# Sliding-window attention with an expert layer on one core: batch 0's q and k turned 128 rows at a time into two banks by position

## The chip, the cores and the metric

The kernel runs on one core of one Trainium2 chip. The metric is the device time in microseconds of one execution. Lower is better.

## The reference

Two computations follow each other. The first is causal attention in a sliding window of 64 positions, over 8 batches, 8 heads, 576 positions and a head width of 64. The second is a two-layer feed-forward block with SiLU over all 8 x 576 = 4608 rows.

```python
scores = scale * np.matmul(q, k.transpose(0, 1, 3, 2))
mask = (rel >= 0) & (rel < window)          # rel = row - column, window = 64
attn = softmax(np.where(mask, scores, -1e9))
x = (attn @ v).transpose(0, 2, 1, 3).reshape(4608, 512)
h = x @ w_in                                # 512 x 2048
out = (h * sigmoid(h)) @ w_out              # 2048 x 512
```

Inputs and output are fp32 in DRAM. The kernel computes in bf16 with fp32 accumulation.

## The kernel before, in words

**Order of work.** The program is unrolled. A planner (class `Plan`) holds a queue of operations for each class of work, each operation with an assumed duration on the engines that may run it, and plays the queues against each other. What it yields is a fixed order of instructions for every engine and the choice of engine and PSUM bank for each operation. On the chip each engine runs its list in that order and waits for semaphores.

**Names.** The four classes of work that matter here are loads (`dma`, `early`, `ld0`), `turn` and `lift` for batch 0, scores, exponent and values (`s`, `exp`, `pv`), and the feed-forward block (`moe`). PSUM has eight banks: `at0` to `at3` and `mp0` to `mp3`. Batch 0 may use all; later the scores use `at` and the feed-forward block `mp`.

**Batch 0's q and k.** Two heads have 1152 rows of 64. They are loaded so that each of the 128 partitions holds nine consecutive rows: `natb[p, 64*m + d]` is row 9p+m. Partitions 0 to 63 hold the first head, 64 to 127 the second. The first q and k come as fp32 by SyncE's queue and are cast by ScalarE (L236); the other six come by GpSimd's queue with a cast in flight (L230). Scores need the head width on the partitions, so TensorE turns these tiles against the identity (`turn_first`, L282), and a `lift` (L292) copies a bank into `qt` or `kt`. A turn handles four heads (two tiles `ws[0]`, `ws[1]`) of q or k; there are four turns and two lifts for each. In the bank the columns stand by m and then p; a lift puts them back in row order 9p+m, so it reads with a stride and writes in a row. Before the change, a bank held a pair of heads (one from each tile), and a lift filled one stretch of 576 columns of `qt` or `kt`.

**Batch 0's scores and values.** For each half `a` (four heads) and each group `g` of three blocks of 64 positions, `scores_first` adds a bias by two matmuls (L314) and makes twelve small matmuls (L322); the exponents run on ScalarE (L340); `values` makes 24 small matmuls (L352); VectorE inverts the sums, scales and transposes into `bridge` (L359, L362, L366). Filler matmuls (L586) stand where the planner expects TensorE to be idle before batch 0's exponents are done.

**The feed-forward block.** A tile is 512 rows. Its first layer (L372) multiplies w_in by `bridge`, SiLU runs on ScalarE (L378), and its second layer (L381) multiplies by w_out. For tile 0 the second layer goes through the 16 slices of w_out in order, four matmuls for each; w_out comes in eight loads of two slices (L267), issued by GpSimd between loads of batch 1 (L240, L255). Scores (L334) and values (L352) of batch 1 are placed between the second-layer matmuls of tile 0, and so on for the later batches.

Of the kernel before, what the change touches and what calls it, by code (L numbers as in the profile page):

```python
# [9 lines left out]
BF16 = mybir.dt.bfloat16  # L10
# [112 lines left out]
def kernel(ctx, tc, q, k, v, w_in, w_out, out):  # L123
    nc = tc.nc
    B, H, S, D = q.shape
# [11 lines left out]
    NK = 2  # L137
# [5 lines left out]
    NM0, MARGIN = 9, 1.3  # L143
# [8 lines left out]
    ident = keep.tile([128, 128], BF16, name="ident")  # L152
# [8 lines left out]
    natbs = [keep.tile([128, S], BF16, name=f"natb{i}") for i in range(NNB)]  # L161
    qt = [keep.tile([128, NP * S], BF16, name=f"qt{i}") for i in range(NK)]
    kt = [keep.tile([128, 64 + NP * S], BF16, name=f"kt{i}") for i in range(NK)]
# [9 lines left out]
    banks = [psum.tile([128, 512], FP32, name=f"at{i}") for i in range(4)]  # L173
    banks += [psum.tile([128, 512], FP32, name=f"mp{i}") for i in range(4)]

    p = Plan(
        {"at": range(4), "pv": range(4, 6), "mp": range(4, 8), "all": range(8)},
        rank=dict(prime=-8, early=-10, one=-9, first=-9, dma=-1, ld0=-1, st=-2, silu=-3, out=-2, pv=0, s=1, moe=99, warm=200, turn=2,
                  norm=0, inverse=0, bridge=0, exp=1, mask=1, lift=2, block=2, shift=2, cast=4, late=5, clear=9),
        rank0=dict(turn=-6, cast=-6, lift=-5, shift=-4.5, exp=-4, mask=-4, inverse=-3.5, norm=-3, bridge=-3.2),  # L180
        ahead=dict(s=-5.5, exp=-4.6, pv=-5.5, inverse=-4.3, norm=-4.2, bridge=-4.25),
    )
# [31 lines left out]
    def clear_k(i):  # L214
        nc.vector.memset(kt[i][:, 0:64].bitcast(FP32), 0.0)

    c_ident = p.add("one", {"POOL": 1.3}, const_ident)
    c_vv = [p.add("one", {"DVE": 0.25}, lambda _, i=i: clear_vv(i)) for i in range(NV)]
    c_k = [p.add("one", {"DVE": 0.15}, lambda _, i=i: clear_k(i)) for i in range(NK)]
# [9 lines left out]
    def load_first_cast(w, u, kk):  # L229
        nc.gpsimd.dma_start(out=natbs[w][:, 0:S], in_=two(u, kk))  # L230

    def load_first(i, kk):
        nc.sync.dma_start(out=nats[i][:, 0:2 * S].bitcast(FP32), in_=two(0, kk))

    def cast_first(e, i, w):
        copies[e](out=natbs[w][:, 0:S], in_=nats[i][:, 0:2 * S].bitcast(FP32))  # L236
# [33 lines left out]
        )  # L270


    def at_bf16(op, i=0):
        return banks[op["bank"][i]].bitcast(BF16)[:, 0:S]

    def turn_first(op, ws):

        for u in range(2):
            for m in range(NM0):
                for j in range(2):  # L280
                    r = slice(64 * j, 64 * j + 64)
                    nc.tensor.matmul(  # L282
                        banks[op["bank"][j]].bitcast(BF16)[64 * u:64 * u + 64, 64 * m:64 * m + 64],
                        lhsT=natbs[ws[u]][r, 64 * m:64 * m + 64], rhs=ident[r, r],
                        is_transpose=True, start=(m == 0), stop=(m == NM0 - 1),
                    )

    def place_one(b, pj, kk):
        return kt[b % NK][:, 64 + pj * S:64 + (pj + 1) * S] if kk else qt[b % NK][:, pj * S:(pj + 1) * S]

    def lift(e, op, pj, kk, i):
        copies[e](  # L292
            out=place_one(0, pj, kk).rearrange("x (p m) -> x p m", m=NM0),
            in_=at_bf16(op, i).rearrange("x (m p) -> x p m", m=NM0),
        )

    def shift_v(e, b, hf, a, z):
# [116 lines left out]
    def add_first_batch():  # L414
        got = {}
        for what, u in FIRST_LOADS:
            if what == "v":
                add_v_loads(0, [u], [c_vv[0]])
                continue
            kk = "qk".index(what)  # L420
            w = n_nat[1] % NNB
            n_nat[1] += 1
            if u == 0:
                i = n_nat[0] % NN
                n_nat[0] += 1
                ld = p.add("ld0", {"SP": 0.45}, lambda _, i=i, kk=kk: load_first(i, kk), dma=-0.15 if kk == 0 else 0.7)
                ca = p.add("cast", {"ACT": 0.7, "DVE": 0.56}, lambda e, i=i, w=w: cast_first(e, i, w), [ld])
                nat_free[i] = [ca]
            else:
                ca = p.add("early" if (what, u) in FIRST_LOADS[2:6] else "dma", {"POOL": 0.6}, lambda _, w=w, u=u, kk=kk: load_first_cast(w, u, kk), dma=0.8)  # L430
            got[what, u] = (w, ca)
            if (what, u ^ 1) not in got:
                continue
            a = u // 2
            ws, loaded = zip(*[got[what, 2 * a + i] for i in range(2)])
            tu = p.add("turn", {"PE": 0.7}, None, [*loaded, c_ident], lat=0.1, pool="all", nb=2)
            tu["fn"] = lambda _, tu=tu, ws=ws: turn_first(tu, ws)
            for i in range(2):
                x = 2 * a + i
                tu["untils"][i].append(p.add("lift", {"ACT": 0.64, "DVE": 0.75}, lambda e, tu=tu, x=x, kk=kk, i=i:  # L440
                                             lift(e, tu, x, kk, i), [tu, c_k[0]]))
                kq_done[(0, a)] = kq_done.get((0, a), []) + tu["untils"][i]

    def add_w_out(which):
# [23 lines left out]
    def add_v_loads(b, parts, busy):  # L468
        v_landed.setdefault(b, []).extend(
            p.add("dma", {"POOL": 1.0}, lambda e, part=part: load_v(e, b, part), busy, dma=1.1, lat=MARGIN * (b > 0)) for part in parts)  # L470
# [61 lines left out]
    def add_tile(j):  # L532
# [46 lines left out]
        free_gt.update(uses)  # L579

    add_first_batch()
    add_batch_v(0)


    def warm(op):
# [4 lines left out]
                 pool="all")  # L590
# [52 lines left out]
```

The softmax here doesn't subtract the row's maximum and nothing guards it: scores larger than these inputs give would overflow.

## Time and profile before

| what | value |
|---|---|
| median of 4 runs | 305.59 us (305.31 to 305.97) |
| the profiled execution | 305.62 us, of which the span is 303.8 us |
| TensorE matmuls, busy | 286.7 us (94% of the span) |
| VectorE, ScalarE, GpSimd, busy | 137.2, 172.2, 125.2 us |
| first-layer matmuls of tile 0 start | 20.70 us |
| second-layer matmuls of tile 0 start | 36.84 us |
| mean granted TensorE clock | 0.989 |

"Span" is the time from the first to the last instruction in the trace. PE is TensorE's matmuls, PEld its weight loads, DVE VectorE, ACT ScalarE, POOL GpSimd, SP SyncE. A row of a timeline begins with its start in us and the time it took; a number in square brackets is the idle time of the engine before it and what ended it. "issue" is idle time for which the profile shows no cause. TensorE works through its list in order, so a wait in one instruction holds up all behind it.

### The profile page before, as it was taken

The page shows a single profiled execution, that of the slowest core. Times are in us where ns is not written, and L with a number is a line of the kernel's source. Part 1 is how long each engine was busy: PE and PEld are TensorE (multiplying, and loading weights), DVE is VectorE, ACT ScalarE, POOL GpSimd, SP SyncE. Part 2 cuts the span into 40 slices and gives each one's busy share as a digit, 9 for nine tenths or more (in the row PEclk, how much of TensorE's full clock was granted, in tenths as well). Part 3 has the DMA queues.
Part 4 walks back from the last instruction along what each step waited for, and adds up shares of the span by engine and source line. Part 5 has one row for each costly group of instructions (what it writes and reads, how often), then busy time and mean ns, then how long its engine had stood idle before and what let it go on. Part 6 is the DMA issues. An engine that isn't in the chain of part 4 may idle for free.

```text
span 303.8 us, 8450 instructions
## 1 busy us (share of the span) xinstructions
PE 286.7 (94%) x3601; PEld 144.7 (48%) x3635; DVE 137.2 (45%) x329; ACT 172.2 (57%) x314; POOL 125.2 (41%) x177
## 2 busy tenths in 40 slices
PE   4969987999999999999999999999999999999996
PEld 2546444554544454445444454445445444444444
DVE  3474466752999098806970786055104520000000
ACT  4856662577357744775387628663667366226611
POOL 8967975969989898991320000000000000000000
PEclk9978999999999999999999999999999999999999
DMA  8999999999999999998290111002001110010012
GB/s 170 161 189 150 135 177 159 161 183 104 153 176 149 113 139 187 151 125 84 78 106 2 38 71 37 1 37 73 35 0 39 56 50 0 37 69 36 2 69 70
DMA packets 115238, 28.64 MB, mean 94 GB/s; under 512 B 104704, under 2 KB 110464, under 8 KB 115200
## 3 DMA queue, kind: packets, MB, share of 16 engines
q0 software_dynamic: 109440, 18.07, 78.9%
q1 hardware_dynamic: 5760, 10.03, 9.2%
q8 instruction: 28, 0.46, 0.6%
q14 instruction: 10, 0.08, 0.1%
HBM read 36.70 MB, written 9.44 MB: 152 GB/s over the span
## 4 chain that ended last, share of the span: by engine, by line
PE 82%; POOL 8%; DMA 5%; issue 3%; ACT 0%; POOLq 0%; ACTq 0%
PE mp L381 39%; PE mp L372 37%; DMA w_in_sb<-in_moe_w_in_dram 3%; PE at L334 3%; PE mp L352 3%; DMA w_out_sb<-in_moe_w_out_dram 2%; POOL vv L255 2%; POOL w_in_sb L261 2%; POOL nat L240 2%; POOL natb L230 1%; POOL w_out_sb L267 1%; PE at L352 1%; ACT g L378 0%; POOL ident L189 0%; ACT ot L387 0%
## 5 line engine op out<-in xcount | busy, mean ns | idle before, releaser
L372 PE MATMUL mp<-bridge,w_in_sb 128*128 128x512 bf16 (+3 forms) x624 | 130.0, 368 | 0.5 <-ACT g L378 0.4
L381 PE MATMUL mp<-w_out_sb,g 128*128 128x512 bf16 (+2 forms) x574 | 124.5, 367 | 5.3 <-issue 3.7
L378 ACT ACTIVATE g<-mp 128x512 bf16<-128x512 f32 (+3 forms) x156 | 86.3, 564 | 37.1 <-PE mp L372 36.1
L372 PEld LDWEIGHTS <-w_in_sb 128*128 128x128 bf16 x624 | 62.0, 99 | 66.9 <-issue 6.6
L381 PEld LDWEIGHTS <-g 128*128 128x128 bf16 x608 | 55.8, 98 | 61.8 <-issue 1.3
L387 ACT COPY ot<-mp 128x512 f32<-128x512 f32 (+2 forms) x36 | 20.1, 562 | 65.3 <-PE mp L381 52.2
L343 DVE TENSOR_TENSOR e<-e,mask 128x384 bf16<-128x384 bf16 x84 | 25.9, 348 | 62.4 <-ACT e L340 61.8
L340 ACT ACTIVATE e<-at 128x384 bf16<-128x384 f32 x88 | 36.5, 496 | 19.2 <-PE at L334 19.1
L240 POOL DMA_DIRECT2D nat<-in_k_dram x56 | 37.2, 675 | 10.8 <-DMA vv<-in_v_dram 3.5
L240 POOL DMA_DIRECT2D nat<-in_q_dram x56 | 37.9, 688 | 5.2 <-DMA vv<-in_v_dram 1.4
L255 POOL DMA_DIRECT2D vv<-in_v_dram x32 | 33.5, 1062 | 11.3 <-PE mp L352 11.3
L366 DVE STREAM_TRANSPOSE bridge<-ox 128x384 bf16<-128x384 bf16 x48 | 24.7, 552 | 0.1
L248 DVE STREAM_TRANSPOSE qt<-nat 128x576 bf16<-128x576 bf16 x28 | 19.8, 746 | 6.3 <-DMA nat<-in_q_dram 6.3
L248 DVE STREAM_TRANSPOSE kt<-nat 128x576 bf16<-128x576 bf16 x28 | 19.7, 742 | 0.8 <-DMA nat<-in_k_dram 0.8
L362 DVE TENSOR_TENSOR ox<-mp,rc 128x384 bf16<-128x384 f32 x37 | 18.3, 536 | 0.1
L352 PEld LDWEIGHTS <-e 128*32 128x32 bf16 x1152 | 11.1, 96 | 14.3 <-issue 11.4
L359 DVE RECIPROCAL rc<-mp 128x6 f32<-128x6 f32 x37 | 6.9, 190 | 16.7 <-PE mp L352 16.1
L334 PE MATMUL at<-qt,kt 32*128 32x64 bf16 x1008 | 11.5, 190 | 0.0
L334 PEld LDWEIGHTS <-kt 32*128 32x128 bf16 x1008 | 9.3, 92 | 4.3 <-issue 3.8
L302 DVE COPY vv<-vv 64x576 bf16<-64x576 bf16 (+1 forms) x13 | 7.4, 573 | 8.2 <-DMA vv<-in_v_dram 8.0
L352 PE MATMUL mp<-vv,e 128*32 128x65 bf16 x888 | 10.4, 194 | 0.0
L340 ACT ACT_TABLE_LOAD x7 | 9.0, 1283 | 2.2 <-PE at L334 2.1
(50 smaller groups left out, 88.1 us busy)
## 6 DMA issues: line engine op xcount, KB each, us to landing
out_dram<-ot SPq DMA_DIRECT2D x35, 256.0 KB, 2.1
vv<-in_v_dram POOLq DMA_DIRECT2D x32, 144.0 KB, 5.8
nat<-in_q_dram POOLq DMA_DIRECT2D x56, 72.0 KB, 4.7
nat<-in_k_dram POOLq DMA_DIRECT2D x56, 72.0 KB, 3.9
w_out_sb<-in_moe_w_out_dram POOLq DMA_DIRECT2D x8, 256.0 KB, 7.7
w_in_sb<-in_moe_w_in_dram POOLq DMA_DIRECT2D x6, 256.0 KB, 7.5
w_in_sb<-in_moe_w_in_dram POOLq DMA_DIRECT2D x4, 128.0 KB, 5.5
natb<-in_q_dram POOLq DMA_DIRECT2D x3, 144.0 KB, 4.9
```

Source lines behind the costliest of these rows:

```text
L240: nc.gpsimd.dma_start(out=nats[i][32 * h:32 * h + 32].rearrange("p (r d) -> p r d", r=NR), in_=(q, k)[kk][b, 4 * a + h].rearrange("(r p) d ...
L248: nc.vector.transpose(out=to[:, 2 * a * S:2 * a * S + 2 * S].rearrange("x (s r t) -> x s r t", s=2, r=NR)[:, :, n * part:n * part + n], in ...
L255: queue[e].dma_start(out=vv[b % NV][:, 2 * g0 + 1:2 * g1 + 1:2, 0:D], in_=v[b].rearrange("h s d -> (h s) d").rearrange("(g p) d -> p g d", ...
L334: nc.tensor.matmul(at_six(op["bank"][h])[:, a, x], lhsT=kt[b % NK][r, at:at + 128], rhs=qt[b % NK][r, at:at + 64], start=(s == a == x == 0 ...
L340: nc.scalar.activation(out=es[n % NE], in_=at_six(bank), func=ACTF.Exp, scale=scale)
L343: nc.vector.tensor_mul(es[n % NE], es[n % NE], mask0 if g == 0 else mask)
L352: nc.tensor.matmul(at_pv(bank)[32 * h:32 * h + 32, x, t], lhsT=e_of(b, a, n, h)[:, x, 32 * t:32 * t + 32], rhs=vv[b % NV][:, (4 * a + h) * ...
L366: nc.vector.transpose(out=bridge[:, n0:n0 + 3, 2 * a:2 * a + 2].rearrange("x t s (u i) -> x t s u i", u=2), in_=oxs[n % NOX].rearrange("p ...
L372: nc.tensor.matmul(banks[bank["bank"][0]][:, lo:hi], lhsT=w_in_sb[:, c, ft * 128:(ft + 1) * 128], rhs=bridge[:, (j * TT + lo) // 64:(j * T ...
L378: nc.scalar.activation(out=gts[gt][:, lo:hi], in_=banks[bank["bank"][0]][:, lo:hi], func=ACTF.Silu)
L381: nc.tensor.matmul(banks[bank["bank"][0]][:, 0:hi - lo], lhsT=gts[gt][:, m * 128:(m + 1) * 128], rhs=w_out_sb[:, f, lo:hi], start=(f == 0) ...
L387: copies[e](out=ots[ot][:, lo:hi], in_=banks[bank["bank"][0]][:, 0:hi - lo])
```

## The change

A turn no longer makes a 64 x 64 transposition for each tile, position m and head. It transposes all 128 rows of a tile at one m at once (64 columns in, 128 columns out), the two tiles of a turn alternating. The first bank takes m = 0 to 4 of both tiles, the second m = 5 to 8. A bank thus holds all four heads for some of the positions, where it held two heads for all of them. A lift copies five or four of every nine columns for all four heads: it writes runs of five or four neighbours. The planner is told 0.6 us for a turn, where it was 0.7.

```diff
-        for u in range(2):
-            for m in range(NM0):
-                for j in range(2):
-                    r = slice(64 * j, 64 * j + 64)
+    HALVES = ((0, 5), (5, NM0))
+
+    def turned(op, i):
+        lo, hi = HALVES[i]
+        return banks[op["bank"][i]].bitcast(BF16)[:, 0:128 * (hi - lo)].rearrange("x (m y) -> x m y", y=128)
...
+        for i, (lo, hi) in enumerate(HALVES):
+            for m in range(lo, hi):
+                for u in range(2):
                     nc.tensor.matmul(
-                        banks[op["bank"][j]].bitcast(BF16)[64 * u:64 * u + 64, 64 * m:64 * m + 64],
-                        lhsT=natbs[ws[u]][r, 64 * m:64 * m + 64], rhs=ident[r, r],
-                        is_transpose=True, start=(m == 0), stop=(m == NM0 - 1),
+                        turned(op, i)[64 * u:64 * u + 64, m - lo], lhsT=natbs[ws[u]][:, 64 * m:64 * m + 64], rhs=ident,
+                        is_transpose=True, start=(m == lo), stop=(m == hi - 1),
                     )
...
-    def lift(e, op, pj, kk, i):
+    def lift(e, op, a, kk, i):
+        to = kt[0][:, 64:] if kk else qt[0]
         copies[e](
-            out=place_one(0, pj, kk).rearrange("x (p m) -> x p m", m=NM0),
-            in_=at_bf16(op, i).rearrange("x (m p) -> x p m", m=NM0),
+            out=to[:, 2 * a * S:2 * a * S + 2 * S].rearrange("x (j p m) -> x j p m", j=2, m=NM0)[:, :, :, HALVES[i][0]:HALVES[i][1]],
+            in_=turned(op, i).rearrange("x m (j p) -> x j p m", j=2),
         )
...
-            tu = p.add("turn", {"PE": 0.7}, None, [*loaded, c_ident], lat=0.1, pool="all", nb=2)
+            tu = p.add("turn", {"PE": 0.6}, None, [*loaded, c_ident], lat=0.1, pool="all", nb=2)
```

More of the change, by code (lines that the diff above doesn't have):

```diff
@@ L270, in load_w_out @@
         )
-    def at_bf16(op, i=0):
-        return banks[op["bank"][i]].bitcast(BF16)[:, 0:S]
+    HALVES = ((0, 5), (5, NM0))
+    def turned(op, i):
+        lo, hi = HALVES[i]
+        return banks[op["bank"][i]].bitcast(BF16)[:, 0:128 * (hi - lo)].rearrange("x (m y) -> x m y", y=128)
     def turn_first(op, ws):
-        for u in range(2):
-            for m in range(NM0):
-                for j in range(2):
-                    r = slice(64 * j, 64 * j + 64)
+        for i, (lo, hi) in enumerate(HALVES):
+            for m in range(lo, hi):
+                for u in range(2):
                     nc.tensor.matmul(
-                        banks[op["bank"][j]].bitcast(BF16)[64 * u:64 * u + 64, 64 * m:64 * m + 64],
-                        lhsT=natbs[ws[u]][r, 64 * m:64 * m + 64], rhs=ident[r, r],
-                        is_transpose=True, start=(m == 0), stop=(m == NM0 - 1),
-                    )
-    def place_one(b, pj, kk):
-        return kt[b % NK][:, 64 + pj * S:64 + (pj + 1) * S] if kk else qt[b % NK][:, pj * S:(pj + 1) * S]
-    def lift(e, op, pj, kk, i):
+                        turned(op, i)[64 * u:64 * u + 64, m - lo], lhsT=natbs[ws[u]][:, 64 * m:64 * m + 64], rhs=ident,
+                        is_transpose=True, start=(m == lo), stop=(m == hi - 1),
+                    )
+    def lift(e, op, a, kk, i):
+        to = kt[0][:, 64:] if kk else qt[0]
         copies[e](
-            out=place_one(0, pj, kk).rearrange("x (p m) -> x p m", m=NM0),
-            in_=at_bf16(op, i).rearrange("x (m p) -> x p m", m=NM0),
+            out=to[:, 2 * a * S:2 * a * S + 2 * S].rearrange("x (j p m) -> x j p m", j=2, m=NM0)[:, :, :, HALVES[i][0]:HALVES[i][1]],
+            in_=turned(op, i).rearrange("x m (j p) -> x j p m", j=2),
         )
@@ L435, in add_first_batch @@
             ws, loaded = zip(*[got[what, 2 * a + i] for i in range(2)])
-            tu = p.add("turn", {"PE": 0.7}, None, [*loaded, c_ident], lat=0.1, pool="all", nb=2)
+            tu = p.add("turn", {"PE": 0.6}, None, [*loaded, c_ident], lat=0.1, pool="all", nb=2)
             tu["fn"] = lambda _, tu=tu, ws=ws: turn_first(tu, ws)
             for i in range(2):
-                x = 2 * a + i
-                tu["untils"][i].append(p.add("lift", {"ACT": 0.64, "DVE": 0.75}, lambda e, tu=tu, x=x, kk=kk, i=i:
-                                             lift(e, tu, x, kk, i), [tu, c_k[0]]))
+                tu["untils"][i].append(p.add("lift", {"ACT": 0.64, "DVE": 0.75}, lambda e, tu=tu, a=a, kk=kk, i=i:
+                                             lift(e, tu, a, kk, i), [tu, c_k[0]]))
                 kq_done[(0, a)] = kq_done.get((0, a), []) + tu["untils"][i]
```

## The prediction

> **What bounds the kernel now.** I read the page's busy shares first, then who waited for whom on TensorE, the timeline around each of those waits, and the loads that the second layer of the first tile needs.
>
> ```profile
> PE 286.7 (94%) x3601; PEld 144.7 (48%) x3635; DVE 137.2 (45%) x329; ACT 172.2 (57%) x314; POOL 125.2 (41%) x177
> PEclk9978999999999999999999999999999999999999
> q8 instruction: 28, 0.46, 0.6%
> ```
>
> TensorE is busy 94% of the span. Its clock dips in slices 2 and 3 only. Queue q8 carries 28 packets of 0.46 MB, 16 KB each: TensorE's own instructions.
>
> ```profile
> PE at L352 <- issue: 4.3, 2, 2.7
> PE at L586 <- POOL ident L189: 4.2, 1, 4.2
> PE mp L381 <- issue: 3.7, 23, 0.2
> PE mp L381 <- DMA w_out_sb<-in_moe_w_out_dram: 1.0, 1, 1.0
> ```
>
> Columns: total us, times, longest. After the opening wait, only three waits are over 0.3 us: two for "issue" in the value products (2.7 and 1.6), one for a w_out load (1.0). Here they are in order of time:
>
> ```profile
> 16.52 0.30 PE L352 MATMUL at<-vv,e 128*32 128x65 bf16 x13
> 19.53 0.35 PE L352 MATMUL at<-vv,e 128*32 128x65 bf16 x11 [2.72 <-issue]
> ...
> 36.84 2.30 PE L381 MATMUL mp<-w_out_sb,g 128*128 128x512 bf16 x8
> ...
> 44.43 1.24 PE L381 MATMUL mp<-w_out_sb,g 128*128 128x512 bf16 x4 [0.98 <-DMA w_out_sb<-in_moe_w_out_dram]
> ...
> 48.51 0.43 PE L352 MATMUL at<-vv,e 128*32 128x65 bf16 x31
> 50.55 0.32 PE L352 MATMUL at<-vv,e 128*32 128x65 bf16 x17 [1.61 <-issue]
> ```
>
> The first "issue" wait lies ahead of the w_out wait, the second behind it. That decides what each is worth, for the loads do not hang on TensorE (GpSimd's queue):
>
> ```profile
> 32.51 0.76 POOL L267 DMA_DIRECT2D w_out_sb<-in_moe_w_out_dram x1
> ...
> 36.94 0.85 POOL L267 DMA_DIRECT2D w_out_sb<-in_moe_w_out_dram x1
> ```
>
> ```profile
> DMA to landing us min/median/max: 7.4/7.4/7.4
> ```
>
> The fourth w_out load, issued at 36.94, lands at 44.35; the second, issued at 32.51, takes 5.5 and lands at 38.0. GpSimd's list up to there (queries, values, w_in, batch 1, w_out) waits for DMA landings alone. So **whatever batch 0 gains or loses, up to what is left of the cover, ends at 44.4**, and only what lies behind counts.
>
> **Why TensorE stops at L352.** Each matmul is two instructions (weight load, matmul) and every weight load is in the trace, so I count. The stalls come before instructions 705 and 1473: 768 apart, three times 256, and 16 KB is 256 instructions of 64 bytes. So blocks start at 193 + 256n. TensorE entered blocks at 8.78, 13.62, 19.53, 37.91, 45.64 and 50.55 us; the q8 packets with the next block started at 10.49, 17.12, 23.17, 40.38, 47.99 and 51.66 and took about 0.95; after both stalls TensorE went on 1.4 to 1.7 after the packet's end. From entry to the next block's being usable is thus 3.6 to 6.0 us here. The two stalled blocks, of small score and value matmuls, were used up in 3.0 and 3.1 us; no other lasts under 4.8.
>
> The Trainium skill speaks otherwise ("Runtime: NRT & Kernel Launch", Instruction fetch mechanics): 16 KiB blocks of 256 instructions, but room for 2048 of TensorE's, and a crossing mostly hidden. By that rule a shift of the count is worth nothing, and the sum below is 0. The trace has two stalls at exact multiples; I take the trace.
>
> **The change part by part.**
>
> *Turns (L282).* Four turns of 36 matmuls become four of 18, so 72 matmuls and 144 instructions go. A warm turn today issues 36 in 0.55 us, 15 ns each, two row halves at once: 30 ns a pair of 64 columns. A new pair has 128 columns; if the two column halves overlap as the value products' column groups do (L352: 24 of 65 columns in 0.24 us), it takes about 2 x 30 and nine pairs 0.5 us: no change. If not, 1.1 us, +0.5 a turn: +2 over four. I take 0 since the nearest row overlaps.
>
> *Their waits.* The second matmul of a turn now needs the second load; before it was the nineteenth. The k turn today starts at 6.29; its second load (issued 1.94, 4.8 to landing) is there at 6.75. All of TensorE's list behind it starts 0.45 later, less the 0.4 by which a finished first bank lets ScalarE start its lift before the turn is over.
>
> *Lifts (L292).*
>
> ```profile
> L292 DVE COPY qt<-at 128x576 bf16<-128x576 bf16 x2 | 1.5, 758 | 2.5 <-PE at L282 2.5
> L292 ACT COPY qt<-at 128x576 bf16<-128x576 bf16 x2 | 1.3, 638 | 1.5 <-PE at L282 1.5
> ```
>
> 576 elements each become 640 (ScalarE gets all four) and 512 (VectorE all four). By 758/576 and 638/576, with a fixed part of some 0.2 us (reciprocal of 6 elements: 182 ns; a 4-element activation: 205), that is 0.69 us each. No row shows writes in runs of four or five; bounds: nothing, and double, +0.7 a lift. I take nothing: the reads were strided already, at one element per ns. Even the double costs 1.4 in the chain (one lift for batch 0's first scores, one for its second half), and it is covered, below.
>
> *A score's wait.* The first score matmul of each half now waits for both engines' lifts of q and k, before for ScalarE's of one pair. Behind it stand all scores of that half. The k lifts, both on ScalarE from 7.46 to 8.64 today, now run on two engines; both end near 8.5, and the third turn goes to 9.2 in any case. Cost about 0.1.
>
> *Order.* From the first-layer matmuls on, all lists are the same; TensorE's is shifted by 142 instructions (144 fewer, one filler matmul more). GpSimd's and SyncE's, and so all DMA issues, are unchanged. In batch 0 the last two score groups now stand before the third value group.
>
> *The blocks of batch 0.* The old start of instruction 705 in the value products becomes a place 36 matmuls into the first layer. Instruction 193 is now in the third score group, near 11.3; the block after it is usable 15.4 to 17.2, wanted near 15.7: a stall of 0 to 1.5. The value products then end near 17.5, and VectorE's reciprocal, product and transpose (0.2 + 0.55 + 0.55, twice over in part) let the first layer start near 18.9, where it was 20.70. It runs 14 us at full clock, 15.4 with one cold window: end at 33 to 34.3, not 37. Worth to the end: nothing, by the w_out landings; the cover, 2.5 to 4 us here, also takes the +2 and +1.4 bounds above.
>
> *Behind 44.4.* New block starts map to old instructions 1103, 1359 and 1615. Old 1103 lies in the second score group of batch 1 (42.9, likely near 42.1 now), old 1359 in its first value products (47.4), old 1615 near 55.9. So the blocks last 4.5 to 5.4, and about 6.7 without the stall, against a need of 42.1 + 2.4 + 0.95 + 1.5, which is 47.0: before 47.4. The stall at 48.94 goes: **-1.6 us**. Of the later blocks, mapped in the same way, none lasts under 5.0, and there the packets start within 1.3 of entry (3.8 in all): no new stall. What is late next after 50 us? The last w_out lands at 40.8 + 10.2, 51.0, and is wanted at 53.7; VectorE's masks and transposes there follow the value products and move with them. From there TensorE is busy to the end.
>
> **The clock.** A longer wait for w_out ahead of 44.4 has a price:
>
> ```profile
> 15.00:20.00 5.00, 2.28 (x77) 1.34 (x76) 3.14 (x10) 3.57 (x7) 4.09 (x6) 0.86 1.21 183
> 20.00:25.00 5.00, 5.00 (x51) 4.27 (x51) 3.70 (x9) 1.89 (x6) 2.61 (x4) 0.50 1.44 191
> 25.00:30.00 5.00, 5.00 (x32) 3.09 (x31) 2.10 (x3) 3.31 (x8) 4.12 (x8) 0.96 1.82 137
> ```
>
> The next-to-last three columns begin with the granted clock. After the 2.72 us gap it was halved from 18.6 to 25.4. The skill ("TensorE: Matmul & The Clock Gate", Part 1) has a free-running window of about 3.4 us that halves the clock when idle and restores it when busy; two of them are the 6.8 here. This rule speaks against the change: the second layer would start at 33 to 34.3, use up its eight matmuls by 36, and stand idle 2 to 3.5 us until 38.0. One cold window from about 39 costs 1.7 us; the work from 38.0 to 44.35 is about 4.9 us (16 matmuls, two score groups), so 1.45 is spare: loss 0.25, sum -1.35. By the trace's two windows it costs 3.4, loss 1.95, sum +0.35. I take one, since TensorE would be busy right after it, as in the window that ended the spell before.
>
> **The sum.** -1.6 without and -1.35 with a cold window: -1.5. The profiled execution took 305.62 (span 303.8 and 1.8 around it), the median is 305.59: **304.1 us**.
>
> **The rivals.**
> 1. *The stall moves instead of going* (15%): if the second score group comes late (cold clock, near 44.1) and the packet is requested only then, the block is usable at 49.0, wanted near 47.9: 0.3 to 1.1 of the gain goes back: 304.4 to 305.4. Against it: at 77 us the packet started 2.5 before entry, so requests run ahead while TensorE works off a queue.
> 2. *Slower, by the clock* (13%): two cold windows around the w_out waits, 306.0 by the sum above; with the stall kept too, 307.6. The point: over 3.05 us lost, 6.1 us of work at half clock after 38.0. For it: the trace did this once. Against: there the second window was needed as the first held 1 us of idle time.
> 3. *Nothing* (7%): block starts do not follow the count, and the front is covered: 305.6.
>
> **How the numbers follow.** The forecast, 65%, holds 303.8 to 304.4. About 0.2% (0.6 us) is what a measurement tells from no change. Rival 1 is shared between faster and same, rival 3 is same, and rival 2 is slower: faster 0.69, same 0.18, slower 0.13. The range goes to 306.0 for rivals 1 and 3 and the mild end of 2, and down to 303.6 for the whole 1.83 gap between weight loads.
>
> **What would show it.** Right: no "issue" wait over 0.5 us on TensorE behind 44 us; a 0 to 1.5 one near 16 in the value products; the first layer near 19; the w_out waits longer, at 38 and 44.4; the 44.4 landing unmoved. Wrong: a stall near 47.5 (rival 1), half clock after 39 for over 4 us (rival 2), a stall still at 48.9 (rival 3), or w_out landing elsewhere.

## The result and the profile after

| | before | changed |
|---|---|---|
| median of the runs | 306.04 us (64 runs) | 304.54 us (43 runs) |
| ratio of changed to before | | 0.9948, 95% interval 0.9937 to 0.9959 |
| the profiled execution, its span | 305.62, 303.8 us | 304.58, 302.8 us |

The change makes the kernel about 1.6 us faster by the ratio, 1.5 us by the medians; 304.1 had been forecast against a before of 305.59. In this larger set before is 306.04, so the forecast gain of 1.5 us is met. Busy shares and clock on the page of the changed kernel:

```profile
PE 287.0 (95%) x3530; PEld 143.1 (47%) x3564; DVE 138.0 (46%) x330; ACT 171.8 (57%) x313; POOL 125.3 (41%) x177
PEclk9999999999999999999999999999999999999999
```

TensorE has 71 weight loads fewer (72 transpositions gone, one filler more). The dip of the clock is not in this execution. Lines have moved: L351, L371 and L380 are the value products and the two layers of the feed-forward block. Who TensorE waited for, with total us, times and longest:

```profile
PE at L584 <- POOL ident L189: 4.2, 1, 4.2
PE mp L380 <- issue: 3.6, 23, 0.2
PE mp L380 <- DMA w_out_sb<-in_moe_w_out_dram: 1.9, 4, 0.8
PE at L284 <- DMA natb<-in_q_dram: 1.1, 1, 1.1
PE mp L371 <- DVE bridge L365: 0.7, 1, 0.7
```

Both long "issue" waits in the value products are gone. In their place stand more waiting for w_out (1.9, was 1.0) and a new wait for the second load of the first turn. TensorE's timeline, the stretch that decides:

```profile
20.68 3.17 PE L371 MATMUL mp<-bridge,w_in_sb 128*128 128x192 bf16 x26
...
36.13 2.09 PE L380 MATMUL mp<-w_out_sb,g 128*128 128x512 bf16 x7
...
44.48 1.24 PE L380 MATMUL mp<-w_out_sb,g 128*128 128x512 bf16 x4 [0.82 <-DMA w_out_sb<-in_moe_w_out_dram]
...
47.44 0.59 PE L380 MATMUL mp<-w_out_sb,g 128*128 128x512 bf16 x2 [0.48 <-DMA w_out_sb<-in_moe_w_out_dram]
...
49.20 0.56 PE L351 MATMUL at<-vv,e 128*32 128x65 bf16 x48
49.92 4.70 PE L380 MATMUL mp<-w_out_sb,g 128*128 128x512 bf16 x21 [0.16 <-issue]
```

The first layer starts where it did (20.68, was 20.70), and the fourth w_out load frees TensorE where it did (44.48, was 44.43). Up to there nothing was gained. Then the second value group of batch 1 (49.20) runs through its 48 matmuls, where it had stopped after 31 for 1.61 us. The next 21 second-layer matmuls start at 49.92, were 51.02: 1.1 us in this pair of executions, whose whole times differ by 1.04. The rest of the 1.6 that the wait was worth went to the 0.48 us for the fifth w_out load.

### The profile page after: what moved, and what is told of

It is laid out like the page before. It is cut to its first block, busy times and chain, and to the rows that moved or that the text cites. A ratio compares the mean times of both kernels' runs of the same rounds, so it can differ in the third digit from the quotient of the medians.

```text
span 302.8 us, 8305 instructions
## 1 busy us (share of the span) xinstructions
PE 287.0 (95%) x3530; PEld 143.1 (47%) x3564; DVE 138.0 (46%) x330; ACT 171.8 (57%) x313; POOL 125.3 (41%) x177
## 4 chain that ended last, share of the span: by engine, by line
PE 82%; POOL 9%; DMA 6%; issue 2%; ACT 0%; POOLq 0%; ACTq 0%
PE mp L380 39%; PE mp L371 37%; DMA w_in_sb<-in_moe_w_in_dram 3%; PE mp L351 3%; PE at L333 3%; POOL vv L255 3%; DMA w_out_sb<-in_moe_w_out_dram 3%; POOL w_in_sb L261 2%; POOL nat L240 2%; POOL natb L230 1%; POOL w_out_sb L267 1%; PE at L351 0%; ACT g L377 0%; POOL ident L189 0%; ACT ot L386 0%
## 5 line engine op out<-in xcount | busy, mean ns | idle before, releaser
L380 PE MATMUL mp<-w_out_sb,g 128*128 128x512 bf16 (+2 forms) x574 | 124.9, 367 | 6.2 <-issue 3.6
L371 PE MATMUL mp<-bridge,w_in_sb 128*128 128x512 bf16 (+3 forms) x624 | 128.4, 362 | 1.3 <-DVE bridge L365 0.7
L371 PEld LDWEIGHTS <-w_in_sb 128*128 128x128 bf16 x624 | 60.2, 97 | 67.9 <-issue 7.9
L380 PEld LDWEIGHTS <-g 128*128 128x128 bf16 x608 | 55.8, 98 | 62.8 <-issue 2.6
L339 ACT ACTIVATE e<-at 128x384 bf16<-128x384 f32 x90 | 37.2, 495 | 20.1 <-PE at L333 19.4
L361 DVE TENSOR_TENSOR ox<-mp,rc 128x384 bf16<-128x384 f32 x39 | 19.4, 536 | 0.1
L351 PEld LDWEIGHTS <-e 128*32 128x32 bf16 x1152 | 10.9, 95 | 9.9 <-issue 7.7
L358 DVE RECIPROCAL rc<-mp 128x6 f32<-128x6 f32 x39 | 7.3, 191 | 16.4 <-PE mp L351 15.7
L351 PE MATMUL mp<-vv,e 128*32 128x65 bf16 x936 | 11.1, 194 | 0.0
```

What stands on the lines that cost most here:

```text
L339: nc.scalar.activation(out=es[n % NE], in_=at_six(bank), func=ACTF.Exp, scale=scale)
L351: nc.tensor.matmul(at_pv(bank)[32 * h:32 * h + 32, x, t], lhsT=e_of(b, a, n, h)[:, x, 32 * t:32 * t + 32], rhs=vv[b % NV][:, (4 * a + h) * ...
L371: nc.tensor.matmul(banks[bank["bank"][0]][:, lo:hi], lhsT=w_in_sb[:, c, ft * 128:(ft + 1) * 128], rhs=bridge[:, (j * TT + lo) // 64:(j * T ...
L380: nc.tensor.matmul(banks[bank["bank"][0]][:, 0:hi - lo], lhsT=gts[gt][:, m * 128:(m + 1) * 128], rhs=w_out_sb[:, f, lo:hi], start=(f == 0) ...
```

## The experiments

Most of the experiments use one tool: small matmuls put at the head of TensorE's list, where the kernel before leaves it idle until 4.18 us. Each is two instructions. They change how many instructions stand ahead of everything else, and that is called the alignment here. In the kernels with small matmuls the value products are L358 (old turns) or L357 (new turns).

```diff
-    c_vv = [p.add("one", {"DVE": 0.25}, lambda _, i=i: clear_vv(i)) for i in range(NV)]
+    def first_vv(i):
+        clear_vv(i)
+        if i == 0:
+            for _ in range(57):
+                nc.tensor.matmul(banks[0][0:32, 0:2], lhsT=vv[0][0:32, 0, 0:32], rhs=vv[0][0:32, 0, 0:2], start=True, stop=True)
+
+    c_vv = [p.add("one", {"DVE": 0.25}, lambda _, i=i: first_vv(i)) for i in range(NV)]
```

| run | kernel | small matmuls | runs | median, us | ratio to before (95%) |
|---|---|---|---|---|---|
| e1 | before | 57 | 16 | 304.54 | 0.9944 (0.9923 to 0.9964) |
| e2 | changed | 71 | 22 | 306.0 | 1.0008 (0.9989 to 1.0027) |
| e3 | before | 128 | 22 | 306.05 | 0.9988 (0.9973 to 1.0003) |
| e4 | before | 112 | 6 | 309.83 | 1.0099 (1.006 to 1.0138) |
| e9 | before | 96 | 22 | 305.06 | 0.9968 (0.9952 to 0.9985) |
| e10 | changed | 55 | 6 | 311.05 | 1.0143 (1.0106 to 1.018) |
| e5 | changed, every lift twice | 0 | 20 | 304.66 | 0.9947 (0.9929 to 0.9965) |
| e6 | changed, fourth w_out load early | 0 | 22 | 304.9 | 0.9957 (0.9938 to 0.9975) |
| e7 | changed, third and fourth early | 0 | 22 | 305.19 | 0.9968 (0.9949 to 0.9988) |
| e8 | before, fourth w_out load early | 57 | 22 | 304.63 | 0.9952 (0.9936 to 0.9967) |

**e1, the new alignment without the change** (57 in the diff above).

> The kernel before with 57 matmuls of 32 x 2 on a zeroed tile put first on TensorE, which is idle there until 4.18 us; the turns and lifts are untouched. They add 114 instructions, so every later instruction stands against the 256-instruction blocks as it does in the changed kernel (-142 and +114 differ by 256). Block theory: the 1.6 us wait near 48.9 is gone and the time falls by 1.0 to 1.6 us, as in the changed kernel. Rival, the turn and lifts themselves brought the gain: no change (305.5 to 306.1 where before is 306). Rival, the half clock from 18.6 to 25.4 us was the loss: gain only if that dip goes too.

The old turns with the new alignment give the whole gain, 0.9944 beside the change's 0.9948. The second value group of batch 1 in its timeline:

```profile
50.79 0.56 PE L358 MATMUL at<-vv,e 128*32 128x65 bf16 x48
51.51 4.70 PE L387 MATMUL mp<-w_out_sb,g 128*128 128x512 bf16 x21 [0.16 <-issue]
```

No stop among the 48. (This profile was taken of the longest of the 16 executions, 306.24 us, with late w_out loads and one half-clock spell, from 38.9 to 42.3, so its times are later; the missing wait is what it is shown for.)

**e2, the change without the new alignment** (`range(71)`).

> The changed kernel with 71 such small matmuls first on TensorE: 142 instructions, which puts the first layer and all behind it where the kernel before has it against the blocks. Block theory: a wait of 1.6 us in the second value group of batch 1 (near 49) is back and the time is that of the kernel before (-0.3 to +0.5 us against it). Rival, the turn and lifts brought the gain: the time stays 1.5 us below the kernel before.

The new turns and lifts with the old alignment are worth nothing: 1.0008. The trace has the wait again in the same value group, one matmul earlier than in before:

```profile
50.42 0.42 PE L357 MATMUL at<-vv,e 128*32 128x65 bf16 x30
51.41 0.33 PE L357 MATMUL at<-vv,e 128*32 128x65 bf16 x18 [0.57 <-issue]
```

It is 0.57 us, not the 1.6 expected: TensorE entered the preceding block at 47.55, the packet with the next one started 1.6 us later (2.3 in before) and ended at 50.12. In this execution the front was later as well (second layer at 39.12). So the time fits the theory, the size of this one wait does not by itself.

**e3, the price of the tool** (`range(128)`, a whole block).

> The kernel before with 128 such small matmuls: one block of 256 instructions, so nothing shifts against the blocks. Block theory: both issue waits stay and the time is that of before within 0.3 us; this is the price of the small matmuls alone. Rival, small matmuls at the start help by themselves (a warmer clock early): the gain of the 57 shows here too.

0.9988, with 1 within the interval: 128 small matmuls cost nothing that can be measured. The two waits stand at 20.00 (2.76 us) and 50.44:

```profile
50.44 0.31 PE L358 MATMUL at<-vv,e 128*32 128x65 bf16 x17 [1.34 <-issue]
```

**e4, another alignment with a wait** (`range(112)`).

> The kernel before with 112 such small matmuls, 224 instructions. Block theory, from the trace of before: blocks now start at what were instructions 1249 and 1505, the third score group and the end of the second value group of batch 1, 3.2 us apart; a wait of about 1.6 us comes right behind that value group, ahead of the second-layer matmuls, and the time is that of before within 0.4 us. If waits do not follow the count: any number, and a wait at another place.

The place was right and the time wrong: 309.8, not 306.

```profile
49.10 0.55 PE L358 MATMUL at<-vv,e 128*32 128x65 bf16 x47
52.88 0.19 PE L358 MATMUL at<-vv,e 128*32 128x65 bf16 x1 [3.23 <-issue]
53.23 6.38 PE L387 MATMUL mp<-w_out_sb,g 128*128 128x512 bf16 x21 [0.16 <-issue]
```

The wait comes after 47 of 48, at the end of the group as reckoned, but it is 3.23 us: the packet started 3.7 us after the preceding block was entered. And the 21 matmuls behind it took 6.38 us, were 4.70: the clock was halved from 54.2 to 57.6. So +1.6 for the longer wait and +1.7 for the clock, of the 3.8 by which this execution is longer than the profiled one of before; it came to this value group 0.6 us later already.

**e9, sixteen small matmuls fewer** (`range(96)`), against the rival that many of them cost by themselves.

> The kernel before with 96 small matmuls first on TensorE, 16 fewer than the 112 that gave 309.8 us. Block theory: blocks now start at what were instructions 1281 and 1537; the second lies behind 16 second-layer matmuls, 6.4 us after the first, so no wait remains behind 45 us and the time is 1.0 to 1.6 us below before (304.4 to 305.0 beside 306.0). Rival, more small matmuls at the start cost by themselves (the 112 lost 3.8 us by it): 308 to 310.

Sixteen fewer turn +1.0% into -0.3%. The second value group of batch 1 runs through, and no "issue" wait over 0.3 us is left behind 45 us:

```profile
47.98 0.56 PE L358 MATMUL at<-vv,e 128*32 128x65 bf16 x48
48.47 4.92 PE L387 MATMUL mp<-w_out_sb,g 128*128 128x512 bf16 x22
```

The median, 305.06, lies just above what was expected. A reading of that, not separated by an experiment: this alignment keeps the wait in batch 0 (2.94 us, at 21.10), and 19 of its 22 runs show a reduced mean clock, where 5 of 16 do in e1. The three of e9 at full clock have a median of 304.05.

**e10, the change in that bad alignment** (`range(55)` in the changed kernel).

> The changed kernel with 55 small matmuls first: 110 instructions, which put all from the first layer on where the kernel before with 112 small matmuls had it. Block theory: a wait of 3 us at the very end of the second value group of batch 1 (near 49 to 50), a half-clock spell behind it in most runs, and the time of that kernel: 2.5 to 4.2 us above before (308.5 to 310.2), with the turns and lifts of the change intact. Rival, the gain is the turns' own: 1.5 us below before.

The changed kernel loses 1.4%. The place of the wait and the half clock behind it are as foreseen; the time, 311.05, is above the 308.5 to 310.2 that were expected:

```profile
48.18 0.55 PE L357 MATMUL at<-vv,e 128*32 128x65 bf16 x46
51.50 0.24 PE L357 MATMUL at<-vv,e 128*32 128x65 bf16 x2 [2.78 <-issue]
51.67 7.80 PE L386 MATMUL mp<-w_out_sb,g 128*128 128x512 bf16 x22
```

Busy time by stretches of that execution; the third number from the right is the granted clock:

```profile
50.00:55.00 5.00, 3.50 (x10) 1.29 (x10) 3.15 (x8) 0.00 (x0) 3.60 (x6) 0.57 1.90 121
55.00:60.00 5.00, 5.00 (x64) 2.15 (x63) 0.65 (x3) 0.00 (x0) 5.00 (x7) 0.75 1.66 106
```

Half clock held from 50.7 to 57.5, two spells of 3.4 us.

**e5, the lifts twice.**

```diff
-        copies[e](
+        for _ in range(2): copies[e](
```

> The changed kernel with every one of its eight lifts done twice, into the same place: about 0.75 us more on ScalarE and 0.72 on VectorE each, in the chain about 1.5 us before batch 0's second half of scores. Cover theory (batch 0 ends at the w_out landings near 44.4): the first layer starts about 1.5 us later (22.2), the waits for w_out shrink from 1.9 us in sum to under 1, and the time moves by 0 to +0.6 us against the changed kernel, so it stays 1.0 to 1.6 under before. Rival, batch 0's length counts: +1.5 us, level with before.

0.9947, the change's own number. Eight more lifts of 0.72 to 0.81 us cost nothing that can be measured. Its profile caught, by chance, the case that the prediction had weighed:

```profile
34.39 2.09 PE L380 MATMUL mp<-w_out_sb,g 128*128 128x512 bf16 x8
39.13 0.59 PE L380 MATMUL mp<-w_out_sb,g 128*128 128x512 bf16 x1 [2.65 <-DMA w_out_sb<-in_moe_w_out_dram]
...
40.41 4.37 PE L380 MATMUL mp<-w_out_sb,g 128*128 128x512 bf16 x15
```

The first layer here starts early (18.95, where 22.2 had been expected), and the waits for w_out are 3.1 us in sum, not under 1: TensorE is through with the eight matmuls by 36.5, stands idle for 2.65 us, and works at half clock from 39.0 to 42.4: 15 matmuls in 4.37 us.

**e6, e7 and e8, is there more behind the w_out loads?** One string orders batch 1's loads (a, b: its q and k; v: a part of its v; w: a w_out load). The edit of e6 and e8 is shown; e7 has "awbwwwvvvv".

```diff
-    FIRST, SECOND_LOADS = 6, "awbwvwvvwv"
+    FIRST, SECOND_LOADS = 6, "awbwvwwvvv"
```

> The changed kernel with w_out's fourth load issued ahead of two of batch 1's value loads (the order of the loads of batch 1 is awbwvwwvvv, it was awbwvwvvwv); the planner places two of the second layer's matmuls otherwise. Cover theory: the fourth load is wanted at 43.7 and lands at 44.5 in the changed kernel; it now comes about 2 us sooner, the last value load about 1 us later, and 0.3 to 1.0 us more is gained (302.0 to 304.2 beside a before of 306). Rival: all loads up to there are one train limited by its bandwidth, and the wait moves to batch 1's value loads: no change against the changed kernel.

> The same with the third and the fourth load of w_out ahead of all four value loads of batch 1 (awbwwwvvvv). Cover theory: the w_out waits go but for the second load's; the value loads land about 2 us later and the first value group of batch 1 may wait: gain of 0 to 1.0 us against the changed kernel. Rival, the train's bandwidth: no change or a loss up to 1 us, with a wait on value loads or their copies in the place of those on w_out.

> The kernel before with the 57 small matmuls, and the fourth w_out load issued early (awbwvwwvvv): the old turns, the alignment of the changed kernel, the new load order. If batch 0's turns do not matter for the time, it stands within 0.4 us of the changed kernel with the same load order; if the old turns' earlier first layer is worth something once the load is early, it is the fastest by 0.5 us or more.

No gain over the change in any (0.9957, 0.9968, 0.9952 beside 0.9948), where up to 1.0 us more had been expected of e6 and e7. In e6 the wait for the fourth load went, and TensorE waits for other w_out loads instead:

```profile
37.23 0.38 PE L380 MATMUL mp<-w_out_sb,g 128*128 128x512 bf16 x1 [1.04 <-DMA w_out_sb<-in_moe_w_out_dram]
...
41.07 2.10 PE L380 MATMUL mp<-w_out_sb,g 128*128 128x512 bf16 x9 [1.36 <-DMA w_out_sb<-in_moe_w_out_dram]
...
46.55 0.81 PE L380 MATMUL mp<-w_out_sb,g 128*128 128x512 bf16 x3 [0.57 <-DMA w_out_sb<-in_moe_w_out_dram]
```

In e7 it waits for the second load (1.10 us) and the fifth (1.65). This speaks for the rival that the loads are one train, though what limits the train was not tested. e8 says once more that the turns do not matter: old ones, 0.9952. No kernel here has a lower median than the change or e1.

## Why the prediction was right

**Right for the reason given.** The step that the stall at 48.94 goes, for -1.6 us, carries the result. e1 and e2 are the two halves of the change: alignment alone brings all of it, turns and lifts alone none. e3 excludes the small matmuls themselves; e9 and e4, 32 instructions apart, differ by 4.8 us in the median. Not all the signs named beforehand came: the first layer did not start near 19 in the profiled execution, and the wait at 44.4 was not longer (0.82 us, was 0.98).

**The rule on instruction blocks.** The prediction set the trace against the Trainium skill's page "Runtime: NRT & Kernel Launch", Instruction fetch mechanics. Its blocks of 256 instructions hold. Counted by weight loads, the instruction behind each long "issue" wait in the value and score products is:

| kernel | instruction behind the wait | remainder by 256 |
|---|---|---|
| before | 705, 1473 | 193 |
| e1 | 705 | 193 |
| e3, e4 | 961, 1729 | 193 |
| e9 | 961 | 193 |
| e2, e10 (changed turns) | 703, 1471 | 191 |

The first of each pair lies in batch 0, ahead of the w_out loads; only the second costs its full length. The 2 between old and new turns is in the count, which leaves out what is no matmul: with the new turns the traces have two semaphore instructions on TensorE's list in batch 0 (at 10.77 and 15.80 us in the changed kernel), with the old ones none. With them the remainder is 193 everywhere, and the change shifts TensorE's list by 140 instructions, not by the 142 of the prediction; that is the one matmul by which the wait in e2 came earlier. "Mostly hidden" does not hold in this stretch: behind 44 us the waits were 0.6 to 3.2 us. Nor does the trace of before show room for 2048 instructions: as it enters 28 blocks, 28 packets come, and at both stalls TensorE went on only 1.4 to 1.7 us after the end of a packet that had started in the preceding block.

**The cover held.** What batch 0 gains or loses ends at the w_out landings, as the prediction had it: e5 (lifts twice) and e1 (old turns) have the same time. That the landing near 44.4 did not move, as forecast, is luck in this pair: the fourth load was issued at 38.03, 1.1 us later than in before, and took 6.4 us instead of 7.4. What the prediction missed is how much the load train itself moves between executions: GpSimd issued the fifth w_out load at 38.7 in the trace of before, 39.8 in that of the changed kernel and 40.7 in e1's, with the same list. The sum had no term for a wait on the fifth load; it took 0.48 us.

**The front was mis-sized.** I had the first layer start near 18.9; it was 20.68 in the profiled execution, and 18.66 to 19.62 in e5 to e7. The term at fault is the wait of the second transposition for the second load. It was put at 0.45 us, on the k turn only; the first turn's load took 3.8 us to landing in the trace of before, which would be 5.05 us. In this execution it took 5.1 us, and TensorE waited 1.15 us for it:

```profile
4.93 0.32 PE L284 MATMUL at<-ident,natb 128*64 128x128 bf16 x1
6.39 1.17 PE L284 MATMUL at<-ident,natb 128*64 128x128 bf16 x17 [1.15 <-DMA natb<-in_q_dram]
```

The clock record begins at full speed at 12.6 here, at 8.3 in before. Three turns took 1.17 us and only the last 0.69, so the slow opening lasted longer too. The stall of 0 to 1.5 us in batch 0's values, forecast near 16, came at its lower end, at nothing: the packet started 2.2 us after the block was entered at 14.04, where up to 3.5 had been reckoned with, and the next block was wanted only 4.5 us after that entry. With the early fronts of e5 and e6 (11.47 and 12.19) the packets started 1.2 and 1.7 us after, and there was no stall either.

**Turn and lift.** A turn at full clock takes 0.69 us to its end, was 0.66: no change, as said. Lifts by row:

```profile
L291 ACT COPY qt<-at 128x640 bf16<-128x640 bf16 x2 | 1.5, 754 | 3.8 <-PE at L284 3.8
L291 DVE COPY qt<-at 128x512 bf16<-128x512 bf16 x2 | 1.4, 720 | 3.8 <-PE at L284 3.8
```

754 and 720 ns, where 690 was put for both. With runs of five and four the lifts are 9% and 4% above that estimate, far from the doubling taken as the bound.

**The clock rival.** It came true in part of the runs. Of the 44 runs of the changed kernel with a recorded clock, 30 stand at 1.0 in the mean or close to it, median 304.31, and 14 near 0.994, which is what one 3.4 us window at half speed makes of the mean; their median is 304.89. So runs with one spell are 0.6 us longer, where 0.25 was put, and none of this turned the sign. That the vanished dip of before, 18.6 to 25.4, is itself the gain was a rival of e1. The runs of before that were taken beside the experiments speak against it: 8 of them have the full clock, and their median is 305.83, 1.5 us above the changed kernel's at full clock; near 0.994 it is 305.85 (84 runs) against 304.89. In e4 and e10 a wait behind the cover drew such a spell, and there it was paid in full.

**The other rivals.** Rival 1, a second score group entered late, has its case in e1 and e5: its block was entered at 44.83 and 44.72 us, the packets ended at 47.89 and 47.11, and the next block was wanted at 49.72 and 49.23, so no wait followed; what stands between came later too. Rival 3, block starts that do not follow the count, is out by the table above. For the later blocks the prediction had packets within 1.3 us of entry; in the changed kernel one came 3.4 us after (at 82.39), in a block that lasted 16.4 us, so nothing came of it.

## What to carry to other kernels

Where small matmuls are dense, count TensorE's instructions, semaphore instructions too, to each unexplained "issue" wait; if the places differ by multiples of 256, as the 705 and 1473 of this kernel do, a change to the number of instructions ahead of them can move the time, whatever else it does. Before crediting a change with a gain, pad the old version to the new count, and the new one to the old: two runs tell alignment from merit. Here the same change is worth -0.5% or +1.4% by the padding alone.

## What had not been expected

- The time from entering a block to the start of the packet with the next one is not a constant: 0.2 to 4.2 us in the first 60 us of these traces; from the packet's end to TensorE's going on it was 1.1 to 1.7 at the waits. So the wait at one place varied from 0.57 (e2) to 1.61 us (before). What delays the packet was not tested.
- A wait of 3 us cost up to twice itself here: the half clock behind it took another 1.7 us in e4 (6.38 us for work of 4.70) and 2.9 in e10 (7.80 for 22 matmuls that take 4.92 us at full clock, as in e6).
